# Scores of k over sixteen places of the array, v loaded in smaller pieces, and a new order table

## The chip, the cores and the metric

The kernel runs on one core of a Trainium2 chip. The metric is device time in microseconds for one execution. Before the change it is 266.17 us, the median of 3 runs (265.9 to 266.24). The engines are named as the profile names them: PE (TensorE's matmuls), PEld (its weight loads), DVE (VectorE), ACT (ScalarE), POOL (GpSimd) and SP (SyncE, which here only issues DMAs).

## The reference

Two layers follow one another. First a Nystrom attention over q, k and v, each of 8 batches, 8 heads, 576 tokens and 64 dimensions; then a normalised two-layer MLP with a residual.

```python
q_lm = q.reshape(B, H, 32, 18, D).mean(axis=3)      # 32 landmarks
k_lm = k.reshape(B, H, 32, 18, D).mean(axis=3)
A, Bm, C = sm(q, k_lm), sm(q_lm, k_lm), sm(q_lm, k)  # softmax of scaled scores
Z = Bm^T / (norm_1(Bm) * norm_inf(Bm))
for _ in range(6): Z = 2 * Z - Z @ Bm @ Z
x = (A @ Z @ C @ v)                                  # heads side by side: 576 x 512
out = x + relu(layernorm(x) * g @ w1) @ w2           # w1: 512 x 2048, w2: 2048 x 512
```

## The kernel before, in words

**Units, sets and streams.** A unit is four heads of one batch, so a batch has two (u = 0, 1). Batch 0 has a path of its own. The others come in sets, each a `Coming` object (line 816): (1,), (2,), (3,4), (5,6) and (7,). In a set the units are numbered w = 0, 1, ..., and two neighbours form a pair: one pair in a set of one batch, two in a set of two. For each set q, k and v are loaded by SP into `stg` tiles (line 917; a ring of six tiles), cast to 16 bits by POOL or ACT into `nat` or `natv` (line 924), turned by DVE into `xT` (line 965) and summed to landmarks `lm`. Then `attention2` (line 1082) runs: landmark products and scores of k (`products_k`, line 1022, tiles `psb` and `psec`), their exponentials by ACT and a transpose by DVE (`scores_k`, line 1041, tiles `ec` and `ecT`), scores of q (`scores_q`, line 1058, tile `psea`), the product of the scores of k with v (line 1125, tile `pscv`), six steps of the iteration for Z, a chain of small matmuls and DVE instructions over the tile `st` (lines 750 and 780), and the normalisation of `ea` by POOL (line 561). The MLP's first layer is cut in 16 chunks a batch (line 1361; four matmuls into `psh`, emptied by ACT or DVE into `hT`); the second layer sums products into `bank` tiles (from batch 4 on by a scheme of seven half-size products, line 1528, with mixed weights `w2mix`).

**Places.** A matmul of 32 rows by 32 columns takes one of sixteen places of the 128 x 128 array, given by its row strip (`rb`) and its column strip (`cb`). The row strip is where the data lie; the column strip is where the result is put in PSUM's partitions, and the kernel may choose it if what reads the result agrees. Matmuls in different places can run beside each other; in one place they follow one another. In `products_k` strip p of unit w goes to column strip p if w is even and to (p + 2) mod 4 if it is odd, for both values of r (lines 1030 to 1038). In `scores_q` the column depends on r too, and x is the outermost loop.

**Loads of v.** The unit with even w is loaded by one DMA (`load`, line 315). The one with odd w (sets after (1,)) is loaded by three (`load_swapped`, line 322): 128 rows for slot 0 and two of 64 rows for slot 1, so that the two halves of the partitions are exchanged. SP's queue also carries the stores of finished blocks (line 1269), and each DMA uses one of eight semaphores in turn.

**Order.** The program is laid out by a planner that runs while it is built. `Clock` (line 85) guesses when each instruction would end; `run` (line 1774) picks the next step among five streams: 0 attentions, 1 totals, 2 first layers, 3 first rows, 4 second layers. `help_out` (line 1646) puts in side work: 5 jobs (DVE's turns and sums), 6 measuring, 7 centering of w1, 8 and 9 mixing of matrices, 10 casts, 11 loads. The table `AFTER` (line 1715) overrules the guesses: `(0, 17): (4, 30)` means that step 17 of the attentions waits until the second layers have taken 30 steps. Each engine executes its instructions in the order thus fixed.

Of the kernel before, what the change touches and what calls it, by code (L numbers as in the profile page):

```python
# [10 lines left out]
FP32 = mybir.dt.float32  # L11
UINT32 = mybir.dt.uint32
AF = mybir.ActivationFunctionType
ALU = mybir.AluOpType
AX = mybir.AxisListType

P = 128
# [3 lines left out]
def kernel(  # L21
# [12 lines left out]
    B, H, S, D = q.shape  # L34
# [4 lines left out]
    LM = 32  # L39
# [4 lines left out]
    NJ = 9  # L44
# [11 lines left out]
        name=nc.get_next_instruction_name(), act_func_set_id=6, ins=[], outs=[]))  # L56
# [28 lines left out]
    class Clock:  # L85
# [71 lines left out]
        def note(self, i):  # L157
            e = str(i.engine).rsplit(".", 1)[-1]
            outs = [a.bass_ap for a in i.outs if hasattr(a, "bass_ap")]
            ins = [a.bass_ap for a in i.ins if hasattr(a, "bass_ap")]  # L160
            size = [[k for _, k in a.ap] for a in outs + ins]
            count = []
            for dims in size:
                n = 1
# [4 lines left out]
            writes = [n for a in outs for n in keys_of(a)]  # L169
            ready = 0.0  # L170
            for n in reads:
                t, who = self.wrote.get(n, (0.0, e))
                if who != e or e != "PE":
                    ready = max(ready, t + (self.WAY if who != e else 0.0))
                if n.startswith("psm"):
                    t, who = self.used.get(n, (0.0, e))
# [7 lines left out]
            if type(i).__name__ == "InstDMACopy":  # L184
                start = max(self.free[e], ready)
                self.free[e] = start + (580 if e == "SP" else 100)
                half_ = size[0][0] == 64 and any(n.startswith("stg") for n in writes)
                self.wire = (max(start + 1650, self.wire)
                             + count[0] * size[0][0] * 4 / (150.0 if half_ else 385.0))
                self.loads = self.loads[-24:] + [(start, self.wire)]  # L190
# [61 lines left out]
    def keep(ins):  # L252
        tc.keep_in_program_order(ins)
        clock.note(ins.ins)
        return ins
# [38 lines left out]
    stage = Ring(name="stage", bufs=6)  # L294
# [27 lines left out]
    def load_swapped(src, b, u, queue):  # L322
        t = stage.tile([P, 2, NJ, D], FP32, name="stg", tag="stg")
        heads = src[b, 4 * u:4 * u + 4].rearrange("h (t j) d -> h t j d", j=NJ)
        keep(queue.dma_start(out=t[:, 0, :, :], in_=heads[1:3].rearrange("h t j d -> (h t) j d")))
        for e in range(2):
            keep(queue.dma_start(out=t[ts(1 - e, 64), 1, :, :], in_=heads[3 * e]))
        return t

    raw, nat_tiles, natv_of = {}, {}, {}  # L330
# [7 lines left out]
    for u in range(U):  # L338
# [21 lines left out]
        out=pairs16[:], in_=pm16[:].rearrange("p (e l) -> p e l", e=2)[:, :, None, :]  # L360
# [358 lines left out]
    def softmax_of(psb, W, whole_=False):  # L719
        rsum = asm.tile([P, W], FP32, name="rsum", tag="rsum")  # L720
        dve.tensor_reduce(out=rsum[:], in_=psb[:], axis=AX.X, op=ALU.add)
        rcr = asm.tile([P, W], FP32, name="rcr", tag="rcr", bufs=1)
        dve.reciprocal(out=rcr[:], in_=rsum[:])
        st = asm.tile([P, W, (5 if whole_ else 2) * LM], FP16, name="st", tag="st")
        dve.tensor_tensor(out=st[:, :, -LM:], in0=psb[:],
                          in1=rcr[:, :, None].broadcast_to([P, W, LM]), op=ALU.mult)
        bmT = asm.tile([P, W, LM], FP16, name="bmT", tag="bmT")
        dve.transpose(bmT[:], st[:, :, -LM:])
        if whole_:
            dve.tensor_tensor(  # L730
                out=st[:, :, 0:P].rearrange("p w (h l) -> p w h l", l=LM),
                in0=bmT[:, :, None, :].broadcast_to([P, W, 4, LM]),
                in1=heads_of[0][:, None, :, None].broadcast_to([P, W, 4, LM]), op=ALU.mult)
        return st, bmT

    def whole_gram(psse_, st):
# [79 lines left out]
    class Coming:  # L816
# [100 lines left out]
        def load(self, i, queue=nc.sync):  # L917
            nm, w = self.parts[i]
            b, u = self.units[w]
            src = {"q": q, "k": k, "v": v}[nm]  # L920
            self.stg[i] = stage.pin(load_swapped(src, b, u, queue) if nm == "v" and self.swapped(w)
                                    else load(src, b, u, queue))

        def cast(self, i, by_act=False, part=None):
# [94 lines left out]
                    self.lm[nm, 2 * y + x] = lm[:, ds(4 * i + 2 * x, 2), :, :].rearrange(  # L1019
                        "p r h (l x) -> p r (h l) x", x=2)  # L1020

    def products_k(pair, lm, xT, psb):
        tiles = {w: ps2.tile([P, 2, 512], FP32, name="psec", tag="p2") for w in pair}
        for w in pair:
            for x in range(2):
                for p_ in range(4):
                    rows, r = ts(p_, 32), p_ % 2
                    MM(psb[rows, w, :], lm["q", w][rows, r, :, x], lm["k", w][rows, r, :, x],
                       rb=32 * p_, cb=32 * p_, start=(x == 0), stop=(x == 1), skip=True)
        for r in range(2):  # L1030
            for x in range(2):
                for w in pair:
                    for p_ in range(4):
                        rows = ts(p_, 32)
                        cb = 32 * ((p_ + 2 * (w % 2)) % 4)
                        MM(tiles[w][ds(cb, 32), r, 0:NJ * LM], lm["q", w][rows, r, :, x],
                           xT["k", w][rows, r, :, :, x], rb=32 * p_, cb=cb,
                           start=(x == 0), stop=(x == 1), skip=True)
        return tiles
# [42 lines left out]
    def attention2(bs, c):  # L1082
        units, lm, xT = c.units, c.lm, c.xT
        W = len(units)
# [9 lines left out]
        for y in range(W // 2):  # L1094
            pair = (2 * y, 2 * y + 1)
            yield lambda: clock.both(0.0 if mine else banks.next(), clock.calm(64), aexp.next("e", 4),
                                     clock.at(*c.lm_tiles[y], *[xT["k", w] for w in pair]))
            if y == 0:
                psb = p1([P, W, LM], "psb")
            tiles = products_k(pair, lm, xT, psb)  # L1100
            if y == W // 2 - 1:
                act(psb[:], psb[:], AF.Exp, scale=sc_B)
                st, bmT = softmax_of(psb, W, whole_)
            ecT[pair[0]], ecT[pair[1]] = scores_k(pair, tiles)
            aprep.unpin(*[xT["k", w] for w in pair])
            for w in pair:
                aexp.pin(ecT[w])
# [538 lines left out]
    def help_out(hurry=False):  # L1646
# [66 lines left out]
    begun_first = [0]  # L1713

    AFTER = {
# [14 lines left out]
    }  # L1730
    taken = [0] * 12
    JOB, MEASURE, CENTER, MIX, MIX_W2, CAST, LOAD = range(5, 12)
# [137 lines left out]
```

## Time and profile before

| | |
|---|---|
| median of the runs | 266.17 us |
| the profiled execution | 266.21 us |
| its span (first to last instruction on the core) | 264.5 us |
| busy: PE, DVE, ACT, POOL | 253.4, 207.8, 172.7, 136.9 us |
| scores of k, `psec` | 224 matmuls, 7 pairs |
| scores of q, `psea` | 224 matmuls, 7 pairs |
| DMAs that load v, sets (1,) to (7,) and batch 0 | 10 whole, 6 of 128 rows, 12 of 64 rows |
| DMA, mean over the span | 176 GB/s |

The span is what the profile's views cover; the execution's time holds 1.71 us more. Rows of the view by time give start, length, engine, line, operation, output and inputs, shape and count. A PE row's end is modelled, and matmuls overlap, so the start of the next instruction is the better mark of what a group costs. Nearly all instructions carry line 302 or 308, the helpers that record them, so they are told apart by the names of their tiles. The granted clock of TensorE was 1.00 throughout.

### The profile page before, as it was taken

Reading aid. Unit: us, or ns where it says so; the run is one execution under the profiler, and the core shown is the slowest. Engines: PE = TensorE matmul, PEld = TensorE weight load, DVE = VectorE, ACT = ScalarE, POOL = GpSimd, SP = SyncE. Lnnn points to the kernel's source line nnn. Section 1 sums busy time; section 2 is a strip of 40 time slices with the busy share of each in tenths; the row PEclk is TensorE's granted clock in tenths of the full one; section 3 lists DMA queues with packets and bytes.
Section 4 is the critical chain, followed back from the end, with each engine's and each line's share of the span. In section 5 each row is a group of like instructions: output and inputs, shape, how many; then the busy total and the mean of one; then the engine's idle time right before and its main releaser. Section 6 shows DMA issues by size and latency. Waiting matters only on the chain.

```text
span 264.5 us, 8154 instructions
## 1 busy us (share of the span) xinstructions
PE 253.4 (96%) x3351; PEld 167.9 (63%) x3351; DVE 207.8 (79%) x465; ACT 172.7 (65%) x333; POOL 136.9 (52%) x163
## 2 busy tenths in 40 slices
PE   7799988999899999999999999999999999999994
PEld 6545754556355674446655556677877875788883
DVE  2567964999979987988997974969798758977662
ACT  2488986548686987478787777677576845864000
POOL 5188779999572889989999915600000005000000
PEclk9999999999999999999999999999999999999999
DMA  7999999999794899965803011110060006100605
GB/s 249 372 398 377 387 388 388 346 327 285 251 304 136 272 332 365 266 211 147 267 12 72 11 43 32 42 40 4 0 160 1 4 22 144 39 0 2 159 17 184
DMA packets 23565, 46.67 MB, mean 176 GB/s; under 512 B 2404, under 2 KB 2664, under 8 KB 23528
## 3 DMA queue, kind: packets, MB, share of 16 engines
q1 hardware_dynamic: 23048, 45.49, 53.2%
q10 hardware_dynamic: 480, 0.66, 0.7%
q8 instruction: 26, 0.43, 0.6%
q14 instruction: 11, 0.09, 0.1%
HBM read 36.70 MB, written 9.44 MB: 174 GB/s over the span
## 4 chain that ended last, share of the span: by engine, by line
PE 81%; DVE 10%; DMA 3%; ACT 2%; issue 1%; SPq 1%; DVEq 0%
PE bank L308 54%; PE psh L308 21%; DMA stg<-in_k_dram 3%; DVE m L302 2%; PE pscv L308 2%; DVE w L302 2%; PE psd L308 2%; DVE xblk L302 1%; DVE six L302 1%; PE psea L308 1%; PE psec L308 1%; DVE part L302 1%; ACT lns L302 1%; DVE xT L302 1%; DVE st L302 1%
## 5 line engine op out<-in xcount | busy, mean ns | idle before, releaser
L308 PE MATMUL bank<-w,hT 128*128 128x512 f16 (+3 forms) x528 | 109.7, 334 | 0.0
L302 ACT ACTIVATE hT<-psh 128x576 f16<-128x576 f32 x121 | 75.7, 654 | 24.0 <-PE psh L308 22.7
L308 PEld LDWEIGHTS <-hT 128*128 128x128 f16 x656 | 61.0, 98 | 31.2 <-issue 6.4
L308 PE MATMUL psh<-ea,m 128*128 128x288 f16 x512 | 78.7, 286 | 0.4 <-DVE ea L302 0.3
L308 PEld LDWEIGHTS <-m 128*128 128x128 f16 x512 | 49.0, 98 | 19.7 <-issue 2.8
L302 DVE SCALAR_TENSOR_TENSOR xblk<-bank,rstd,xblk 128x256 f32<-128x256 f32 (+2 forms) x77 | 39.0, 541 | 12.5 <-PE bank L308 12.4
L302 POOL TENSOR_TENSOR ea<-ea,lns 128x576 f16<-128x576 f16 x14 | 17.9, 1285 | 52.0 <-ACT lns L302 51.4
L302 POOL CAST nat<-stg 128x1152 f16<-128x1152 f32 x24 | 27.9, 1182 | 8.9 <-DVE xT L302 6.8
L302 POOL CAST natv<-stg 128x1152 f16<-128x1152 f32 (+1 forms) x17 | 19.3, 1162 | 14.7 <-DMA stg<-in_v_dram 8.1
L302 DVE BATCH_NORM_STATS2 six<-xblk 128x6 f32<-128x512 f32 x36 | 24.2, 674 | 1.6 <-ACT xblk L302 1.6
L302 DVE STREAM_TRANSPOSE xT<-nat 128x576 uint32<-128x576 uint32 x28 | 21.3, 760 | 0.0
L302 DVE SCALAR_TENSOR_TENSOR st<-st,bank 128x128 f16<-128x128 f16 (+3 forms) x36 | 13.2, 366 | 9.6 <-PE bank L308 9.2
L302 ACT COPY xblk<-bank 128x512 f32<-128x512 f32 (+1 forms) x29 | 16.6, 593 | 3.4 <-PE bank L308 2.7
L308 PE MATMUL bank<-w2mix 128*128 128x256 f16 x128 | 17.9, 273 | 0.0
L308 PE MATMUL bank<-w2mix,hT 128*128 128x256 f16 x128 | 16.1, 273 | 0.0
L302 ACT CAST m<-bank 128x512 f16<-128x512 f32 x16 | 9.3, 590 | 8.8 <-PE bank L308 8.7
L302 ACT ACTIVATE lns<-psd 128x576 f32<-128x576 f32 x16 | 10.3, 646 | 7.3 <-PE psd L308 7.1
L308 PEld LDWEIGHTS <-st 32*32 32x32 f16 (+1 forms) x380 | 6.9, 90 | 12.3 <-DVE st L302 7.7
L302 DVE TENSOR_REDUCE part<-xT 128x32 f16<-128x576 f16 x20 | 14.3, 742 | 0.2
L308 PE MATMUL bank<-zcbd,ea 128*128 128x256 f16 x80 | 14.2, 273 | 0.0
L302 POOL TENSOR_TENSOR asum<-nat 128x512 f32<-128x512 f16 x10 | 12.3, 1226 | 3.2 <-ACT nat L302 2.6
L308 PEld LDWEIGHTS <-w2mix 128*128 128x128 f16 x128 | 12.4, 98 | 2.1 <-issue 0.2
(130 smaller groups left out, 369.1 us busy)
## 6 DMA issues: line engine op xcount, KB each, us to landing
stg<-in_q_dram SPq DMA_DIRECT2D x16, 576.0 KB, 6.4
stg<-in_k_dram SPq DMA_DIRECT2D x16, 576.0 KB, 6.0
out_dram<-xblk SPq DMA_DIRECT2D x66, 128.0 KB, 2.4
wstg<-in_moe_w_ch_dram SPq DMA_DIRECT2D x16, 512.0 KB, 7.6
stg<-in_v_dram SPq DMA_DIRECT2D x10, 576.0 KB, 7.4
stg<-in_v_dram SPq DMA_DIRECT2D x6, 288.0 KB, 5.9
stg<-in_v_dram SPq DMA_DIRECT2D x12, 144.0 KB, 5.5
out_dram<-xblk ACTq DMA_DIRECT2D x4, 128.0 KB, 2.9
```

The source lines that it names most:

```text
L302: return lambda *args, **kw: keep(getattr(self.engine, op)(*args, **kw))
L308: keep(nc.tensor.matmul(o, l, r, start=start, stop=stop, tile_position=(rb, cb), skip_group_check=(skip or cb != 0)))
```

## The change

Three things change. In `products_k` the loops over r and x change places, for all sets; and in the sets from (3,4) on ("turned") the column strip is also moved by r, so that a pair uses all sixteen places. The partitions in which the scores of slot r = 1 land are then other ones, so v's slot 1 is loaded to match, in pieces of 32 rows: a unit with u = 0 by five DMAs (one of 128 rows, four of 32), one with u = 1 by six (two of 64 rows, four of 32). In the two sets that iterate on whole 128 x 128 matrices, (2,) and (7,), the mask that spreads the softmax into a block-diagonal matrix is `mask4` (heads in order) in place of `heads_of[0]` (heads 1 and 2 exchanged). The planner's clock takes DMAs of 32 rows as slow ones, as it does those of 64, and `AFTER` is replaced: 72 entries in place of 59, 13 of them the same as before.

```diff
-                half_ = size[0][0] == 64 and any(n.startswith("stg") for n in writes)
+                half_ = size[0][0] <= 64 and any(n.startswith("stg") for n in writes)
...
+    TURNED = 3
+
+    def load_turned(src, b, u, queue):
+        t = stage.tile([P, 2, NJ, D], FP32, name="stg", tag="stg")
+        heads = src[b, 4 * u:4 * u + 4].rearrange("h (t j) d -> h t j d", j=NJ)
+        if u == 0:
+            keep(queue.dma_start(out=t[:, 0, :, :], in_=heads[0:2].rearrange("h t j d -> (h t) j d")))
+        else:
+            for e in range(2):
+                keep(queue.dma_start(out=t[ts(e, 64), e, :, :], in_=heads[1 - e]))
+        for e in range(2):
+            rows, slot = (64 * e, 1) if u == 0 else (64 * (1 - e), e)
+            for half in range(2):
+                keep(queue.dma_start(out=t[ds(rows + 32 * half, 32), slot, :, :],
+                                     in_=heads[2 + e][ds(32 * (1 - half), 32)]))
+        return t
...
-                in1=heads_of[0][:, None, :, None].broadcast_to([P, W, 4, LM]), op=ALU.mult)
+                in1=mask4[:, None, :, None].broadcast_to([P, W, 4, LM]), op=ALU.mult)
...
-            self.stg[i] = stage.pin(load_swapped(src, b, u, queue) if nm == "v" and self.swapped(w)
+            self.stg[i] = stage.pin(load_turned(src, b, u, queue) if nm == "v" and self.bs[0] >= TURNED
+                                    else load_swapped(src, b, u, queue) if nm == "v" and self.swapped(w)
                                     else load(src, b, u, queue))
...
-        for r in range(2):
-            for x in range(2):
+        for x in range(2):
+            for r in range(2):
                 for w in pair:
                     for p_ in range(4):
                         rows = ts(p_, 32)
-                        cb = 32 * ((p_ + 2 * (w % 2)) % 4)
+                        cb = 32 * (p_ ^ 2 * (w % 2) ^ (r if turned else 0))
                         MM(tiles[w][ds(cb, 32), r, 0:NJ * LM], lm["q", w][rows, r, :, x],
                            xT["k", w][rows, r, :, :, x], rb=32 * p_, cb=cb,
                            start=(x == 0), stop=(x == 1), skip=True)
...
-            tiles = products_k(pair, lm, xT, psb)
+            tiles = products_k(pair, lm, xT, psb, bs[0] >= TURNED)
...
-        (0, 95): (2, 110), (0, 104): (4, 513), (0, 112): (4, 558), (0, 116): (4, 584),
+        (0, 45): (4, 153), (0, 64): (4, 196), (0, 80): (4, 267), (0, 95): (4, 335),
+        (0, 99): (4, 463), (0, 104): (4, 513), (0, 112): (4, 559), (1, 5): (4, 94),
...
+        (2, 94): (4, 256), (2, 106): (4, 336), (2, 109): (4, 339), (2, 117): (4, 383),
+        (2, 121): (4, 378), (2, 132): (4, 476), (2, 133): (4, 477), (2, 137): (4, 488),
+        (2, 138): (4, 493), (2, 139): (4, 497), (2, 141): (4, 512), (2, 144): (4, 579),
```

More of the change, by code (lines that the diff above doesn't have):

```diff
@@ L1020, in spread, with products_k @@
                         "p r h (l x) -> p r (h l) x", x=2)
-    def products_k(pair, lm, xT, psb):
+    def products_k(pair, lm, xT, psb, turned):
         tiles = {w: ps2.tile([P, 2, 512], FP32, name="psec", tag="p2") for w in pair}
```

25 rows, old and new, of the table AFTER are left out of this document.

## Prediction, made before the result was known

> **What bounds the kernel now.** I read the page first (busy shares, then the chain that ended last), then the table by stretches of time, then the waits of TensorE's weight loads from 60 us on.
>
> ```profile
> span 264.5 us, 8154 instructions
> PE 253.4 (96%) x3351; PEld 167.9 (63%) x3351; DVE 207.8 (79%) x465; ACT 172.7 (65%) x333; POOL 136.9 (52%) x163
> ...
> PE 81%; DVE 10%; DMA 3%; ACT 2%; issue 1%; SPq 1%; DVEq 0%
> ```
>
> ```profile
> 50.00:75.00 25.00, 23.76 (x264) 13.64 (x263) 24.39 (x48) 17.99 (x35) 21.33 (x24) 1.00 0.91 282
> 75.00:100.00 25.00, 25.00 (x282) 15.55 (x279) 21.78 (x47) 20.10 (x39) 16.52 (x18) 1.00 0.81 269
> 100.00:125.00 25.00, 24.78 (x466) 13.05 (x465) 21.93 (x48) 17.41 (x39) 23.14 (x26) 1.00 0.75 241
> ...
> 200.00:225.00 25.00, 24.98 (x341) 18.38 (x340) 19.01 (x46) 15.34 (x32) 3.56 (x3) 1.00 0.20 47
> ```
>
> ```profile
> PEld L308 <- DVE st L302: 4.7, 11, 1.7
> ```
>
> The columns of the stretches are length, busy PE, PEld, DVE, ACT and POOL (with counts), granted clock, DMA share and GB/s. PE is 96% busy, and 81% of the chain is PE. From 50 to 75 us DVE is the full engine (24.39 of 25 us); from 75 us on PE has hardly a gap, at a granted clock of 1.00. The last row says that in these 200 us the weight loads waited 4.7 us in 11 places for `st`, the chain of small inverse iterations. So a microsecond taken out of PE after 75 us is worth nearly a microsecond, unless it is taken out just ahead of one of those waits.
>
> **The change, part by part: the scores of k.** The five pairs of units that are turned (two of set (3,4), two of (5,6), one of (7,)) run here, `psec` being their tile; the `bank<-lm` rows are the 16 landmark products ahead of them.
>
> ```profile
> 98.79 0.23 PE L308 MATMUL bank<-lm 32*32 32x32 f16 x9
> 98.86 0.30 PE L308 MATMUL psec<-xT,lm 32*32 32x288 f16 x1
> ...
> 98.87 0.30 PE L308 MATMUL psec<-xT,lm 32*32 32x288 f16 x1
> ...
> 98.91 0.68 PE L308 MATMUL psec<-xT,lm 32*32 32x288 f16 x28
> ```
>
> ```profile
> 138.28 0.27 PE L308 MATMUL bank<-lm 32*32 32x32 f16 x16
> 138.39 0.76 PE L308 MATMUL psec<-xT,lm 32*32 32x288 f16 x32
> ```
>
> ```profile
> 201.55 0.77 PE L308 MATMUL psec<-xT,lm 32*32 32x288 f16 x32
> ```
>
> A group of 32 lasts 99.59 - 98.86 = 0.73, 0.76 and 0.77 us. Before, unit w uses the places (p, p) or (p, p^2): eight of the sixteen, four matmuls one behind the other in each. Turned, r moves the column too: sixteen places, two matmuls in each. The trace has that very pattern already: `psea` (the scores of q) is 32 matmuls of the same 32x288 form over all sixteen places, x outermost.
>
> ```profile
> 104.53 0.47 PE L308 MATMUL psea<-xT,lm 32*32 32x288 f16 x32
> ```
>
> ```profile
> 150.63 0.24 PE L308 MATMUL bank<-st 32*32 32x64 f16 x8
> 150.76 0.53 PE L308 MATMUL psea<-xT,lm 32*32 32x288 f16 x20
> ```
>
> Alone it takes 0.47 us. With small matmuls directly ahead it ends at 151.29, 0.66 after the first of these started; for `psec` the same measure is 99.59 - 98.79 = 0.80, and 139.15 - 138.28 = 0.87. So one pair saves between 0.14 (0.80 - 0.66) and 0.30 (0.77 - 0.47). `psec` keeps its small matmuls ahead, but in four places only, and the other twelve are free at once, so I take 0.22, the middle. Five pairs: 5 x 0.22 = **1.1 us**, with ends 0.7 and 1.5. All five lie after 75 us.
>
> The Trainium skill has a rule against this (TensorEngine Tiling (Array Packing), Restrictions and Gotchas, Gotcha 1): different row tiles cannot access the same PSUM bank simultaneously. In `products_k` the four row strips of one unit write one bank, and the first four `psec` matmuls (the first and the last of them are the rows at 98.86 and 98.87) start within 0.02 us of each other, so the trace speaks against it. What it would give is the last rival below.
>
> In sets (1,) and (2,) only the order of r and x changes: the same eight places with four matmuls in each. The exponentials wait for a unit's last matmul either way. I count nothing; the ends are minus and plus 0.1 us, since these two groups lie where DVE is the full engine.
>
> **The mask.** In batches 2 and 7 one operand of one DVE instruction becomes another tile of 128x4 floats, read with the same broadcast.
>
> ```profile
> 203.09 0.43 DVE L302 TENSOR_TENSOR st<-bmT,heads 128x256 f16<-128x256 f16 x1
> ```
>
> Same shape, same type: 0.43 us stay 0.43. Nothing, with ends of 0.05 us either way.
>
> **The loads of v.** For sets from (3,4) on an even unit goes from one DMA to five, an odd one from three to six. Set (3,4) has two of each: 8 issues become 22. Its SP queue and what POOL does with the data:
>
> ```profile
> 71.57 0.55 SPq L317 DMA_DIRECT2D stg<-in_v_dram  x1
> 72.41 0.35 SPq L325 DMA_DIRECT2D stg<-in_v_dram  x1
> 72.81 1.15 SPq L327 DMA_DIRECT2D stg<-in_v_dram  x2
> 74.53 1.13 SPq L1274 DMA_DIRECT2D out_dram<-xblk  x2
> 75.76 0.53 SPq L317 DMA_DIRECT2D stg<-in_v_dram  x1
> 79.39 0.35 SPq L325 DMA_DIRECT2D stg<-in_v_dram  x1
> 79.79 1.14 SPq L327 DMA_DIRECT2D stg<-in_v_dram  x2
> 81.03 1.38 SPq L1274 DMA_DIRECT2D out_dram<-xblk  x2
> 85.26 2.51 SPq L317 DMA_DIRECT2D stg<-in_k_dram  x2
> ```
>
> ```profile
> 87.32 4.49 POOL L302 CAST natv<-stg 128x1152 f16<-128x1152 f32 x4
> 93.25 3.43 POOL L302 CAST nat<-stg 128x1152 f16<-128x1152 f32 x3 [1.45 <-DVE xT L302]
> ...
> 115.75 1.28 POOL L302 TENSOR_TENSOR ea<-ea,lns 128x576 f16<-128x576 f16 x1 [0.24 <-PE bank L308]
> ```
>
> ```profile
> L327 SPq DMA_DIRECT2D stg<-in_v_dram x12: 495/587/1471, 46.0 to 125.9; - x12
> ...
> DMA to landing us min/median/max: 3.3/5.5/8.4
> ```
>
> No DMA of 32 rows is in the trace; the nearest is that of 64 rows, 0.59 us of SP's queue at the median and 5.5 us to its landing. Fourteen more are 14 x 0.59 = 8.3 us of queue. Between 71.57 and the last v issue SP has gaps of 0.3, 0.6, 0.1 and 3.1 us, 4.1 together, so the last piece goes out about 4.2 us later: from 80.4 (79.79 + half of 1.14) to 84.6, and lands at 90.1. POOL's fourth cast of v starts at 87.32 + 3 x 1.12 = 90.7. It fits by 0.6 us. The two stores at 74.53 and 81.03 and the load of k at 85.26 go behind the pieces; the stores are waited for by nobody near, and the k is needed by POOL from 93.25 on. If that cover goes, with the longest landing of 8.4 us, the cast is 2.3 us late, and then the 1.45 us that POOL idled ahead of 93.25 takes most of it. Behind this cast stand POOL's casts and sums and the two normalisations of batch 3, the second at 115.75, whose result PE uses first here:
>
> ```profile
> 121.00 0.65 PE L308 MATMUL psh<-ea,m 128*128 128x288 f16 x4
> ```
>
> That is 121.00 - 117.03 = 4 us later. So up to 1.45 + 4 = 5.4 us of delay costs PE nothing, and beyond it a microsecond costs a microsecond. Set (5,6) has more room: its last v is issued and cast here,
>
> ```profile
> 107.36 1.14 SPq L327 DMA_DIRECT2D stg<-in_v_dram  x2
> ```
>
> ```profile
> 120.26 4.47 POOL L302 CAST natv<-stg 128x1152 f16<-128x1152 f32 x4
> ```
>
> 12 us apart; and the last v issue of all, at 125.9 by the row of L327, is that of batch 7, whose scores run at 201.55. I count the loads at nothing.
>
> **The new table.** It holds no work, only which stream may go on when. Taken against the kernel's own order before, it keeps most steps where they were, holds a few dozen back by one to a dozen steps of the second layer, and frees some. The largest holds are in the first layers (step 117 waits for 15 more second-layer steps, step 139 for 12). A second-layer step is one matmul:
>
> ```profile
> 202.25 1.27 PE L308 MATMUL bank<-w2mix 128*128 128x256 f16 x10
> ```
>
> and ten of them take 1.27 us where one alone lasts 0.27, a pitch of 1.00 / 9 = 0.11 us. Moving it costs PE nothing; only a wait that is opened or closed counts. With PE already full after 75 us there is little to close: some of the 4.7 us above. From both sides I bound it by minus 1 us (a fifth of the 4.7) and plus 2 us (rival 3 with twelve chunks), and take nothing, since the order is mostly the old one.
>
> **Sum.** 264.5 - 1.1 = 263.4 us of span. The profiled execution took 266.21 us, 1.71 more than its span, and the median of the runs is 266.17, the same within 0.02%. 263.4 + 1.7 = **265.1 us**, 0.4% faster; its own range by the ends of the first term is 264.7 to 265.5.
>
> **Rivals.** A measurement of this kernel tells about 0.2% (0.5 us) from no change.
> 1. The saved time is lost in waits for `st`. At 201.55 softmax's DVE chain starts from the landmark products, not from `psec`, and ends at 203.09 + 0.43; PE would arrive 0.22 us sooner and wait as much longer. If three of the five places are like that, 0.4 us remain: 265.8 us. For it: PE waits there now; against it: other products can be put in between. 13%.
> 2. The new order also closes waits, some 0.8 us of the 4.7: 264.3 us. For it: the many one-step moves near the `st` steps; against it: nothing in the trace shows which. 15%.
> 3. Slower: the order bunches first-layer chunks. A chunk takes PE 0.49 us, and the ACT instruction that empties its tile 0.65:
>
> ```profile
> L302 ACT ACTIVATE hT<-psh 128x576 f16<-128x576 f32 x121 | 75.7, 654 | 24.0 <-PE psh L308 22.7
> ```
>
> ```profile
> 208.19 0.49 PE L308 MATMUL bank<-w2mix 128*128 128x256 f16 x3
> 208.51 0.65 PE L308 MATMUL psh<-ea,m 128*128 128x288 f16 x4
> ```
>
> (The chunk's row is 0.65 to its last end; the next instruction starts 0.49 after it.) Two such tiles exist. Now, near 208 us, a chunk has three products of the second layer beside it, and PE does not wait. Held back without them, each chunk costs 0.16 us. Ten bunched chunks (1.6 us) undo the gain and pass the 0.2%; sixteen, a whole batch, give 265.1 + 2.6 = 267.7; at about twelve 267.0. 12%.
> 4. Slower: v too late in set (3,4), the mechanism above. It decides from 5.4 + 1.6 = 7 us of delay on, say 268. 4%, since the sum has it 0.6 us early.
> 5. The change does not do what it says: the four row strips of one bank take turns. A step in a place now takes (0.73 - 0.30) / 3 = 0.14 us; eight in turn per bank last 7 x 0.14 + 0.30 = 1.3 us instead of 0.75, and five pairs lose 2.7: 268.9 us. Against it stand the four starts above. 3%.
>
> **How the numbers follow.** Forecast 53%, and the rest as given. Faster: the forecast, rival 2, and none of rival 1: 68%. Within 0.2%: rival 1 and a little of rival 3: 14%. Slower: what is left of 3, with 4 and 5: 18%. The range leaves out the better part of rivals 4 and 5 and the ends of 2 and 3: 263.9 to 267.0.
>
> **What would show it.** Right: the five `psec` groups at 0.47 to 0.6 us instead of 0.73 to 0.77, first starts in sixteen places, the exponentials following sooner, PE busy as full as before after 75 us, and a span shorter by their sum. Wrong: POOL idle ahead of `natv` for `stg<-in_v_dram` between 85 and 95 us; PE or its weight loads waiting for ACT (`hT`) or longer for `st`; or `psec` groups still at 0.7 us. A span that changes by much more than five groups can explain is the table's doing.

## The result and the profile after

The changed kernel takes **265.53 us** (median of 19 runs, 264.95 to 266.36) against 266.23 for the kernel before on the same chip (19 runs, 265.88 to 267.02): a ratio of 0.9974, with the interval 0.9966 to 0.9982. That is 0.70 us less; forecast were 265.1, or 1.1 less. The profiled execution took 265.93 us, its span is 264.2.

From the page of the changed kernel, the span, the busy shares and the shares of the chain that ended last:

```profile
span 264.2 us, 8212 instructions
PE 253.6 (96%) x3351; PEld 167.7 (63%) x3351; DVE 209.4 (79%) x466; ACT 173.2 (66%) x333; POOL 136.0 (51%) x162
...
PE 75%; DVE 11%; DMA 8%; ACT 2%; POOL 2%; issue 1%; SPq 0%; DVEq 0%
```

Its stretches of time, with the columns as before (length, busy PE, PEld, DVE, ACT, POOL, granted clock, DMA share, GB/s):

```profile
50.00:75.00 25.00, 24.36 (x267) 13.73 (x265) 24.46 (x49) 17.59 (x35) 22.56 (x25) 1.00 0.91 286
75.00:100.00 25.00, 24.90 (x277) 15.49 (x276) 21.67 (x46) 20.50 (x40) 15.86 (x16) 1.00 0.78 251
100.00:125.00 25.00, 25.00 (x480) 13.12 (x478) 22.72 (x50) 18.59 (x39) 21.60 (x24) 1.00 0.71 200
...
150.00:175.00 25.00, 24.07 (x353) 15.26 (x353) 19.29 (x39) 18.42 (x32) 14.26 (x13) 1.00 0.19 44
...
200.00:225.00 25.00, 24.97 (x343) 18.41 (x341) 18.33 (x44) 15.38 (x32) 3.57 (x3) 1.00 0.21 48
```

Before, the fourth of these was:

```profile
150.00:175.00 25.00, 25.00 (x402) 15.55 (x400) 19.13 (x41) 18.06 (x32) 11.50 (x10) 1.00 0.19 44
```

Two of these stretches are not what the sum had. From 50 to 75 us PE is busier (24.36 us, 23.76 before). From 150 to 175 us, where nothing of the change was expected, PE lacks 0.93 us. TensorE's waits from 60 us on say what it waited for, its weight loads first:

```profile
PEld L308 <- DVE st L302: 3.8, 10, 1.0
```

```profile
PE bank L308 <- DVE xblk L302: 0.9, 1, 0.9
```

The weight loads' longest wait for `st` has gone from 1.7 to 1.0 us, and PE's wait for `xblk` is new. The scores of k did what the diff says; here are the first rows of the landmark products and the last row of `psec` in one group each of sets (3,4) and (7,), with the product that follows the latter:

```profile
98.61 0.24 PE L308 MATMUL bank<-lm 32*32 32x32 f16 x9
...
98.72 0.53 PE L308 MATMUL psec<-xT,lm 32*32 32x288 f16 x21
...
201.95 0.24 PE L308 MATMUL bank<-lm 32*32 32x32 f16 x9
...
202.05 0.55 PE L308 MATMUL psec<-xT,lm 32*32 32x288 f16 x22
202.53 0.72 PE L308 MATMUL bank<-w2mix 128*128 128x256 f16 x5
```

The measure of the prediction, from the first of the small matmuls to the last end, is 99.25 - 98.61 = 0.64 us, where it was 0.80; the two parts of the pair overlap as `psea` does.

### The profile page after: what moved, and what is told of

Same layout as the page of the kernel before. It is cut to its first block, busy times and chain, and to the rows that moved or that the text cites. A ratio compares the mean times of both kernels' runs of the same rounds, so it can differ in the third digit from the quotient of the medians.

```text
span 264.2 us, 8212 instructions
## 1 busy us (share of the span) xinstructions
PE 253.6 (96%) x3351; PEld 167.7 (63%) x3351; DVE 209.4 (79%) x466; ACT 173.2 (66%) x333; POOL 136.0 (51%) x162
## 4 chain that ended last, share of the span: by engine, by line
PE 75%; DVE 11%; DMA 8%; ACT 2%; POOL 2%; issue 1%; SPq 0%; DVEq 0%
PE bank L308 49%; PE psh L308 20%; DMA stg<-in_k_dram 4%; DMA wstg<-in_moe_w_ch_dram 4%; DVE m L302 2%; DVE w L302 2%; PE pscv L308 2%; PE psd L308 2%; DVE xblk L302 1%; DVE six L302 1%; DVE part L302 1%; POOL w L302 1%; PE psea L308 1%; ACT lns L302 1%; DVE xT L302 1%
## 5 line engine op out<-in xcount | busy, mean ns | idle before, releaser
L302 ACT ACTIVATE hT<-psh 128x576 f16<-128x576 f32 x119 | 74.3, 653 | 20.9 <-PE psh L308 19.2
L302 POOL CAST nat<-stg 128x1152 f16<-128x1152 f32 x23 | 26.9, 1186 | 12.9 <-DVE xT L302 7.1
L302 POOL TENSOR_TENSOR asum<-asum 128x256 f32<-128x256 f32 (+1 forms) x20 | 12.8, 641 | 1.6
```

The lines of the kernel that those rows point to most:

```text
L302: return lambda *args, **kw: keep(getattr(self.engine, op)(*args, **kw))
```

## The theories and the experiments

The question is whether the 0.70 us are the 1.1 us of the places with a little lost, or a sum of larger parts. Three parts can be set apart: the **places**, the **loads** of v (both together are the **work**), and the **order** that the table makes. The obstacle is that the planner lays out the program by its clock's guesses, so a change of work also changes the order. So in eight of the eleven experiments the clock is shown the other variant: for a product in `products_k`, `clock.seen` holds the place that the clock is to believe, and `unseen(...)` issues loads of one kind while the clock notes the cost of another. The order of the instructions on DVE, ACT and POOL is then exactly that of the kernel before ("old order") or of the changed one ("new order"), and on PE too except inside the groups of the scores of k (one of the eight keeps the order of the run that holds the measuring step). All times are medians. The ratios are to the kernel before on the same chip, which took 266.21 us beside the first four experiments, 266.30 beside the two with the loads of set (7,), the one that holds the measuring step and the one with loops and mask, and 266.19 beside the rest. The changed kernel was timed only in the runs of the result, against 266.23, so a difference to its 265.53 also holds what chips differ by. What a run changes of the computation is said in its expectation.

### Work in the old order, and the new order without the work

**The new places and loads in the old order.** On the kernel before, with its table and its mask, and with the loops over r and x exchanged as in the change:

```diff
-                        cb = 32 * ((p_ + 2 * (w % 2)) % 4)
+                        cb = 32 * (p_ ^ 2 * (w % 2) ^ (r if turned else 0))
+                        clock.seen = (32 * p_, 32 * ((p_ + 2 * (w % 2)) % 4))
...
-            self.stg[i] = stage.pin(load_swapped(src, b, u, queue) if nm == "v" and self.swapped(w)
+            self.stg[i] = stage.pin(unseen(load_turned, src, b, u, queue, "swapped" if self.swapped(w) else "plain")
+                                    if nm == "v" and self.bs[0] >= TURNED
```

> The order of all engines' instructions is that of before; only the places of the scores of k in the five turned pairs and the loads of v are the changed ones (no new table, old mask). Theory A (the gain is the five shorter groups of scores, 0.16 us each in the two profiles, and nothing else adds up): 0.8 us faster than before, ratio 0.9970. Rival B (the new order makes the gain, the saved PE time falls into waits): within 0.2 us of before. Rival C (the smaller pieces of v cost something that the order repays): between 0.8 us faster and no change, and slower than the run with the places alone.

Measured: 265.19 us, ratio 0.9955 (0.9936 to 0.9975). The work alone gives 1.02 us, a little more than theory A has.

**The new places alone in the old order**: the same, without the second hunk.

> As before in order and loads; only the places of the scores of k are changed in the five turned pairs. The second half of v's rows then meets the wrong scores: the product with v is of the same size but not the reference's. Theory A: 0.8 us faster than before. Rival B: within 0.2 us. Rival C: faster than the run with the loads too.

Measured: 266.03 us, ratio 0.9995 (0.9975 to 1.0015): 0.18 us less, and the interval covers no change, so rival B by the time. In the profiled execution the five groups are 0.88 us shorter than before; 0.2 of that go into a longer stop of PE near 111 us and 0.2 into a wait at set (7,), both shown below.

**The new order without the work.** On the changed kernel, with its table and mask, but old places and old loads:

```diff
-                        cb = 32 * (p_ ^ 2 * (w % 2) ^ (r if turned else 0))
+                        clock.seen = (32 * p_, 32 * (p_ ^ 2 * (w % 2) ^ (r if turned else 0)))
+                        cb = 32 * ((p_ + 2 * (w % 2)) % 4)
...
-            self.stg[i] = stage.pin(load_turned(src, b, u, queue) if nm == "v" and self.bs[0] >= TURNED
+            self.stg[i] = stage.pin(unseen(load_swapped if self.swapped(w) else load, src, b, u, queue, "turned")
+                                    if nm == "v" and self.bs[0] >= TURNED
```

> The order of all engines' instructions is that of the changed kernel, with the new mask; the scores of k lie in the eight old places and v is loaded as before. Theory A: the order alone is worth nothing or less (it ends a wait near 70 us and opens one near 171 us): 266.2 to 266.5. Rival B: 265.5, as the changed kernel. In the profile the wait of PE for xblk near 171 us should be there again, about 1 us.

Measured: **265.03 us**, ratio 0.9949 (0.9933 to 0.9966). The order alone gives 1.18 us; with the work that it was made for, the kernel is 0.5 us slower than without. Both expected times missed, and the wait for `xblk` near 171 us, expected here, is not there: it is the changed kernel's. So the work alone is worth 1.02 us and the order alone 1.18, and both together 0.70: the parts do not add up.

**The new order and the new loads with the old places**: the first hunk of that diff alone.

> The changed kernel with the scores of k in the eight old places, v loaded in the new pieces, so that the product with v is of the same size but not the reference's. Theory A: 0.8 us slower than the changed kernel, the same as the run with the old loads too. Rival B: as the changed kernel, 265.5. Rival C: slower than the run with the old loads.

Measured: 265.96 us, ratio 0.9988 (0.9972 to 1.0004): rival C.

What follows: in the new order the loads cost 265.96 - 265.03 = 0.93 us, and the places give 265.96 - 265.53 = 0.43. (In the old order the loads give 266.03 - 265.19 = 0.84, and the places 0.18.) Each of these medians is uncertain by 0.3 to 0.5 us, so the traces have to say where. These are the starts (us) of the `psec` groups from the second on, and the span:

| kernel | 2nd | 3rd | 4th | 5th | 6th | 7th | span |
|---|---|---|---|---|---|---|---|
| before | 67.53 | 98.86 | 101.84 | 138.39 | 142.34 | 201.55 | 264.5 |
| new order, old work | 66.96 | 98.37 | 101.36 | 137.68 | 141.16 | 201.07 | 263.3 |
| new order, new loads, old places | 67.13 | 98.53 | 101.52 | 137.85 | 141.33 | 202.28 | 264.5 |
| changed | 67.27 | 98.68 | 101.50 | 137.87 | 141.19 | 202.01 | 264.2 |

Between the second and the third of these kernels the distance stays at 0.16 or 0.17 us up to the 6th group, and is 1.21 at the 7th: **the loads' cost is one event between 141 and 202 us**, long after the last load of v. It is PE's new wait. Here is PE in the changed kernel, and then in the new order with the old work:

```profile
170.75 0.39 PE L308 MATMUL psm<-w,zt 64*32 64x512 f16 x1
172.07 0.37 PE L308 MATMUL bank<-w,zt 64*32 64x512 f16 x1 [0.93 <-DVE xblk L302]
```

```profile
170.86 0.39 PE L334 MATMUL psm<-w,zt 64*32 64x512 f16 x1
171.13 0.37 PE L334 MATMUL bank<-w,zt 64*32 64x512 f16 x1
```

The second group of eight matmuls follows the first after 0.27 us in one and 1.32 us in the other. `xblk` is written by DVE. DVE and POOL at that place in the changed kernel, and DVE's instructions on `w2mix` there (minimum, median and maximum in ns):

```profile
169.21 2.15 DVE L302 TENSOR_TENSOR w2mix<-hT 128x1024 f16<-128x1024 f16 x2
171.28 0.74 DVE L302 SCALAR_TENSOR_TENSOR xblk<-bank,rstd,xblk 128x512 f32<-128x512 f32 x1
```

```profile
169.78 1.04 POOL L302 COPY hT<-hT 128x1024 f16<-128x1024 f16 x1 [1.47 <-PE bank L308]
```

```profile
L302 DVE TENSOR_TENSOR w2mix<-hT x2: 693/1114/1536, 169.2 to 169.8; 128x1024 f16<-128x1024 f16 x2
```

and the same in the new order with the old work:

```profile
169.12 1.29 DVE L328 TENSOR_TENSOR w2mix<-hT 128x1024 f16<-128x1024 f16 x2
170.33 0.75 DVE L328 SCALAR_TENSOR_TENSOR xblk<-bank,rstd,xblk 128x512 f32<-128x512 f32 x1
```

```profile
169.88 1.44 POOL L328 COPY hT<-hT 128x1024 f16<-128x1024 f16 x1 [1.47 <-PE bank L334]
```

The second of DVE's two mixing instructions takes 1.54 us instead of 0.69, and POOL's copy 1.04 instead of 1.44. In the changed kernel the DVE instruction starts at 169.21 + 2.15 - 1.54 = 169.82, 0.04 us after POOL's copy; in the other at 169.12 + 1.29 - 0.69 = 169.72, 0.16 us before it. Whoever starts first runs at its own speed, and the other is held up: DVE by 0.85 us, or POOL by 0.40. The Trainium skill (SBUF — State Buffer, SBUF: two separate sides) says this: DVE and GpSimd share a pair of ports as an exclusive lock, for a DVE instruction with two inputs in SBUF against a GpSimd instruction that reads SBUF, and the one that starts first has it for the whole instruction. The trace agrees, 1.54 against 0.69 us. The one that is held ends close to where it would if it began at the other's end: DVE at 169.21 + 2.15 = 171.36 against 169.78 + 1.04 + 0.69 = 171.51, and POOL at 169.88 + 1.44 = 171.32 against 169.12 + 1.29 + 1.04 = 171.45.

Why DVE is late by just that much is in its queue ahead of the first mixing instruction. The last statistics instruction there, in the changed kernel, is this:

```profile
168.91 0.18 DVE L302 BATCH_NORM_AGGREGATE stats<-six 128x2 f32<-128x6 f32 x1
```

Instructions that only wait for semaphores, between it and the mixing, in the changed kernel and in the other (count, ns, first and last start):

```profile
L302 DVEq EVENT_SEMAPHORE  x3: 50/50/50, 168.9 to 169.1; - x3
```

```profile
L328 DVEq EVENT_SEMAPHORE  x1: 50/50/50, 169.0 to 169.0; - x1
```

They are 0.10 us apart, so two more are 0.2 us. (In the old order the same waits cost nothing: a copy of 0.69 us stands ahead of them, and the mixing starts 0.61 us after its start with the old loads and with the new.) By the kernel's code, `w2mix` is a tile of the ring `stg` (tag `stg`), and the tile that was there before held v of set (7,). It is now filled by five or six DMAs on semaphores of their own, and the first instruction that writes over it must wait for all of them, some 35 us after the last was issued. That is the theory to test; the rival is that the loads, in flight longer, delay something of set (7,) by themselves.

### Where the loads' cost comes from

**The changed kernel, with the v of set (7,) alone loaded as before:**

```diff
+            self.stg[i] = stage.pin(unseen(load_swapped if self.swapped(w) else load, src, b, u, queue, "turned")
+                                    if nm == "v" and self.bs[0] == 7
```

> The changed kernel in its own order, but v of set (7,) is loaded as before, by one and three DMAs (the second half of its rows meets the wrong scores; all sizes stay). Theory D (the six DMAs of a v tile make DVE wait for each of their semaphores before it writes that tile's buffer again as w2mix; that sets the second mixing instruction behind POOL's copy of hT, DVE is held for 0.8 us, and PE waits 1.0 us for xblk near 171 us): fewer semaphore waits before the first w2mix at 169 us, both mixing instructions together 1.3 us instead of 2.15, no wait of PE near 171 us, 1.0 us faster than the changed kernel, 264.5. Rival E (the wait comes from the loads of the other sets, which move the DMAs and POOL between 70 and 125 us): no difference, 265.5, with the wait.

Measured: 264.62 us, ratio 0.9937 (0.9915 to 0.9959): 0.91 us less than the changed kernel, as theory D has it. Two waiting instructions are left of the three; DVE and POOL:

```profile
168.68 1.29 DVE L328 TENSOR_TENSOR w2mix<-hT 128x1024 f16<-128x1024 f16 x2
```

```profile
169.34 1.53 POOL L328 COPY hT<-hT 128x1024 f16<-128x1024 f16 x1 [1.48 <-PE bank L334]
```

DVE's second instruction starts at 168.68 + 1.29 - 0.69 = 169.28, ahead of the copy at 169.34, and takes 0.69 again. PE does not wait.

**The opposite: the new order and old work, with the v of set (7,) alone in pieces:**

```diff
-                                    if nm == "v" and self.bs[0] >= TURNED
+                                    if nm == "v" and TURNED <= self.bs[0] < 7
```

> The run of the new order with the old work, where only v of set (7,) is loaded in the new pieces (which meet the wrong scores; all sizes stay). Theory D: the wait near 171 us comes back, the mixing pair takes 2.15 us again, and the time goes from 265.0 to 266.0. Rival E: 265.0, no wait.

Measured: 265.17 us, ratio 0.9956 (0.9940 to 0.9972). **The expectation failed**: the wait at PE did not return, though the three waiting instructions did. The rows show why:

```profile
169.71 1.29 DVE L328 TENSOR_TENSOR w2mix<-hT 128x1024 f16<-128x1024 f16 x2
```

```profile
170.31 1.60 POOL L328 COPY hT<-hT 128x1024 f16<-128x1024 f16 x1 [1.48 <-PE bank L334]
```

DVE's second instruction starts at 170.32, 0.01 us after POOL's copy, and still it is POOL that is held (1.60 us). So the three waits put DVE at the edge of the collision, but a few hundredths of a microsecond decide it: 0.01 us late is won, 0.04 us late (the changed kernel, and the one with old places) is lost. By the profile's start times, then, the first to start is not always the one that has the ports. The last statistics instruction starts here at

```profile
169.44 0.18 DVE L328 BATCH_NORM_AGGREGATE stats<-six 128x2 f32<-128x6 f32 x1
```

Counted from its start in each kernel, POOL's copy always comes at the same time, and the waits alone move DVE:

| kernel | waiting instructions | DVE's second mixing, us | POOL's copy, us | held |
|---|---|---|---|---|
| new order, old work | 1 | 0.71 | 0.87 | POOL |
| changed, old loads of (7,) | 2 | 0.81 | 0.87 | POOL |
| old work, new loads of (7,) | 3, one of them of 21 ns instead of 50 | 0.88 | 0.87 | POOL |
| changed | 3 | 0.91 | 0.87 | DVE |
| new order, new loads, old places | 3 | 0.91 | 0.87 | DVE |

So the mechanism of theory D stands, with 0.03 us between won and lost; its forecast for this run failed by the one shorter wait.

**The changed kernel with the measuring step held again.** The old table held measuring step 22 until attention step 96; the new table has no such entry. Measuring is what DVE does right ahead of the mixing: the statistics of a finished block. One entry puts it behind it; the orders of PE, DVE and ACT change by it between 168 and 198 us (36 places of DVE's, 14 of ACT's):

```diff
+        (6, 22): (4, 299),
```

> The changed kernel with one entry more in the table: measuring step 22 waits until the second layers have taken 299 steps (the table before the change held it too), so that DVE mixes w2mix 0.9 us earlier, ahead of POOL's copy of hT. Theory D: no wait of PE near 171 us, 264.4 to 264.8. Rival E: the wait stays, 265.5. If another wait opens in its place, in between.

Measured: **263.95 us**, ratio 0.9908 (0.9879 to 0.9937), less than both kernels and less than expected. DVE, POOL and the stretch from 150 to 175 us:

```profile
167.61 1.28 DVE L302 TENSOR_TENSOR w2mix<-hT 128x1024 f16<-128x1024 f16 x2
...
169.41 0.74 DVE L302 SCALAR_TENSOR_TENSOR xblk<-bank,rstd,xblk 128x512 f32<-128x512 f32 x1
```

```profile
169.19 1.20 POOL L302 COPY hT<-hT 128x1024 f16<-128x1024 f16 x1 [1.47 <-PE bank L308]
```

```profile
150.00:175.00 25.00, 25.00 (x365) 16.36 (x364) 19.30 (x39) 17.97 (x33) 12.16 (x11) 1.00 0.19 44
```

The two mixing instructions are over at 168.89, before POOL's copy starts, with the new loads and all their waits in place, and PE is busy all of the 25 us. So in this order the loads cost nothing by themselves; their cost is the collision. That this edit gives 1.58 us in the medians where the wait is 0.93 is not all explained. Its span is 1.7 shorter, and only 1.12 of that arise between the 6th and the 7th `psec` group, where the edit acts; 0.41 are there already at the 2nd, and 0.18 more arise between the 4th and the 5th, before it has done anything.

**The same with the old places**, to have the worth of the places once more:

```diff
+        (6, 22): (4, 299),
...
-                        cb = 32 * (p_ ^ 2 * (w % 2) ^ (r if turned else 0))
+                        clock.seen = (32 * p_, 32 * (p_ ^ 2 * (w % 2) ^ (r if turned else 0)))
+                        cb = 32 * ((p_ + 2 * (w % 2)) % 4)
```

> The run with measuring step 22 held, where only the scores of k are put back into the eight old places in the five turned pairs (v's pieces then meet the wrong scores; all sizes stay). Theory A, now for the places alone: in an order without the collision the places are worth their five shorter groups, less what the waits take: 0.6 to 0.8 us slower than with the new places, 264.6 to 264.8. Rival B: within 0.2 us, 264.0.

Measured: 265.12 us, ratio 0.9960 (0.9949 to 0.9972), so the places give 1.17 us here, more than expected, in the medians of two chips; the spans are 263.3 and 262.5, 0.8 apart. The starts of the `psec` groups are 67.06, 98.46, 101.45, 137.78, 141.25, 201.09 against 66.86, 98.27, 101.10, 137.29, 140.61, 200.31: the distance is 0.20 and 0.19 up to the first turned pair, then grows by 0.14 to 0.16 with each pair, to 0.78 at the 7th. The 0.20 at the start are scatter of the two executions, so about 0.6 us of the 0.8 are the places'.

### The loops, the mask, the loads and the table by themselves

**The kernel before with the loops exchanged and the new mask:**

```diff
-        for r in range(2):
-            for x in range(2):
+        for x in range(2):
+            for r in range(2):
...
-                in1=heads_of[0][:, None, :, None].broadcast_to([P, W, 4, LM]), op=ALU.mult)
+                in1=mask4[:, None, :, None].broadcast_to([P, W, 4, LM]), op=ALU.mult)
```

> The kernel before with two small parts of the change alone: r and x exchanged in the scores of k (the same eight places) and the new mask in batches 2 and 7. All theories: no change, within 0.2 us of before.

Measured: 266.21 us, ratio 1.0000 (0.9981 to 1.0019). No change, within 0.2%.

**The new loads alone in the old order** (the second hunk of the first experiment alone):

> The kernel before in its own order, where only v of the sets from (3,4) on is loaded in the new pieces (which meet the wrong scores; all sizes stay). Theory F (the pieces stretch SP's issues, so that the DMA engines have a gap near 108 us, PE's next instructions are there in time, and the stop of PE in the product with v near 111 us goes): no stop of PE near 111 us, 0.4 to 0.6 us faster than before, 265.7. Rival C (pieces cost, or do nothing by themselves): as before or slower, with the stop.

Measured: 265.81 us, ratio 0.9999 (0.9980 to 1.0018). The median is 0.38 us less, but the interval covers no change, and the profiled execution was among the longer ones (266.54). This was inconclusive on time. It shows one thing: in the old order PE stops near 111 us, in the product with v, when the loads are the old ones, and does not when they come in pieces. (With loops and mask exchanged the stop is there too, 0.09 us.) The kernel before, then the new places in the old order, then the new loads in the old order:

```profile
111.45 0.60 PE L308 MATMUL pscv<-natv,ecT 64*64 64x130 f16 x28 [0.22 <-issue]
```

```profile
111.28 0.60 PE L334 MATMUL pscv<-natv,ecT 64*64 64x130 f16 x28 [0.43 <-issue]
```

```profile
111.04 1.25 PE L334 MATMUL pscv<-natv,ecT 64*64 64x130 f16 x72
```

The DMA traffic differs just ahead of it. The stretch from 108 to 109 us in the new places in the old order, and in the new places and loads in the old order:

```profile
108.00:109.00 1.00, 1.00 (x47) 0.51 (x19) 0.97 (x3) 0.56 (x2) 0.92 (x2) 1.00 1.10 420
```

```profile
108.00:109.00 1.00, 1.00 (x48) 0.51 (x19) 0.97 (x3) 0.56 (x2) 0.92 (x2) 1.00 0.07 14
```

With the pieces the DMA engines are nearly idle there (0.07 of their time, 1.10 without). So in the old order the pieces remove a stop: from before to the first experiment PE gains 0.41 us at 111 us. "issue" names no releaser. A candidate is in the trace: some of its DMA packets are loads of instructions, 16 KB each, for an engine that it does not name. One ends at 109.81 us in the kernel before and at 109.70 with the new places in the old order, and PE goes on at 111.45 and 111.28, 1.64 and 1.58 us later. With the new loads in the old order it ends at 109.28, and PE passes the place without a stop. That fits instructions which arrive late because the data hold them up, but no run changes that alone, and it is not shown. That the DMA engines are full is not enough by itself, as this stretch of the new order with the old work shows:

```profile
108.00:109.00 1.00, 1.00 (x20) 0.41 (x5) 0.97 (x3) 0.79 (x2) 0.92 (x2) 1.00 1.01 359
```

The DMA engines are nearly as full there, the load of instructions ends at 108.87, and PE does not stop. So the cause stays open; and as the stop is gone in the new order with the old loads as well, the pieces and the order remove the same stop, and it counts only once.

**The changed kernel with the old table** (the order is not kept here; the planner makes its own):

```diff
-        (0, 17): (4, 31), (0, 23): (4, 77), (0, 34): (2, 51), (0, 35): (4, 106),
+        (0, 17): (4, 30), (0, 19): (2, 44), (0, 23): (4, 76), (0, 27): (4, 78), (0, 34): (2, 51),
...
```

> The changed kernel with the table of before: same work as the changed kernel, but the planner, which now counts shorter scores and longer loads, lays it out with entries made for the old work. Theory G (the entries fit only the order they were made for): slower than the changed kernel, by 0.5 us or more, 266.0 to 268. Rival: as the run of the new work in the old order, 265.2.

Measured: 273.23 us, ratio 1.0249 (1.0227 to 1.0271), 7.0 us more than before and past the expected 268. The stretch from 100 to 125 us and PE's longest wait in this kernel:

```profile
100.00:125.00 25.00, 22.16 (x433) 10.28 (x431) 18.39 (x42) 11.00 (x27) 20.60 (x23) 0.93 0.78 238
```

```profile
PE bank L308 <- DVE st L302: 3.9, 4, 1.8
```

PE lacks 2.8 us in that stretch alone, with the granted clock at 0.93. Here the old table does not carry over to the new work.

## Why the prediction was right, and where it was not

The total was right, 265.53 within 263.9 to 267.0 and faster by more than 0.2%; the sum behind it was not. It had one term of 1.1 us. The runs show three, two of which it had at nothing, and that the total came out near the forecast is luck: a gain of 1.18 and a cost of 0.93 nearly cancel.

| step | forecast, us | measured, us |
|---|---|---|
| places, five pairs | -1.1 (-0.7 to -1.5) | groups -0.82; net -0.43 (new order) and about -0.6 (measuring held, spans without the start) |
| loads of v | 0 | +0.93 in the new order, by the collision of DVE and POOL |
| loops, mask | 0 | 0.00 |
| new table | 0 (-1 to +2) | -1.18 |
| sum | -1.1 | -1.18 + 0.93 - 0.43 = -0.68 |

The measured terms are differences from one run to the next, so their sum closes by construction, and they hold for this sequence alone (first the order, then the loads, then the places). In the old order the work as a whole gives 1.02 us, close to the 1.1, but not as the sum had it: by the medians 0.84 of it are the loads', and the places alone give 0.18.

- **Places.** The mechanism was right and the size too large. From the first `psec` start to the next instruction the five groups took 0.65, 0.65, 0.70, 0.65 and 0.70 us before and take 0.50, 0.51, 0.50, 0.51 and 0.51 now: 0.82 us together, 0.16 a pair where 0.22 was taken. (In the new order with the old places they take 0.65 to 0.66, so 0.74 us of it are the places'.) I had taken the middle between the time of `psea` alone and with small matmuls ahead of it; the group is at the second of these (0.66 by the same measure, 0.64 here), so the lower end was the answer. The small matmuls sit in four places only, and still cost as much.
- **Rival 1** (the saved time lost in waits for `st`) is true for one of the five pairs. The new places in the old order, at set (7,):

```profile
201.00 0.54 PE L334 MATMUL psec<-xT,lm 32*32 32x288 f16 x32
...
203.01 0.29 PE L334 MATMUL bank<-st 128*128 128x128 f16 x2 [0.24 <-DVE st L328]
```

  The pair has become 0.22 us shorter, and PE waits 0.24 us at the next step, where it waited 0.02 before (the prediction took it that PE waits there already). In the new order 0.15 us are given back at the same place, against the kernel with the old places. The other four keep their gain there, though one is lost again near 111 us in the profiled execution of the changed kernel, where 16 weight loads for `st` take 0.35 us instead of 0.17.
- **Loads of v.** What was worked out held in its result: the data are there when POOL casts them. SP's queue, and POOL's casts:

```profile
84.75 1.97 SPq L343 DMA_DIRECT2D stg<-in_v_dram  x4
```

```profile
86.97 4.48 POOL L302 CAST natv<-stg 128x1152 f16<-128x1152 f32 x4
```

```profile
stg<-in_v_dram SPq DMA_DIRECT2D x40, 72.0 KB, 3.0
```

  The last piece goes out by 86.7 (84.6 forecast), but a piece takes 1.82 / 4 = 0.46 to 0.49 us of the queue and lands after 3.0 us at the median, not 5.5, so it is there by 89.7 and the fourth cast starts at 86.97 + 3 x 1.12 = 90.3 without a wait. Rival 4 is out. **The step that failed is "I count the loads at nothing"**: it followed the data to their reader, and not the buffer to its next writer, which now waits for six DMA semaphores where the same order with the old loads has it wait for two.
- **The table. The step that failed is "take nothing, since the order is mostly the old one".** Rival 2 was the case, with a size (1.18) past its 0.8 and past the bound of minus 1, which came from the waits for `st` alone. The largest wait that went is this one, in the kernel before; then the stretch from 67 to 75 us before and after:

```profile
70.98 0.19 PE L308 MATMUL bank<-st,bones 128*128 128x64 f16 x1 [0.69 <-DVE st L302]
```

```profile
67.00:75.00 8.00, 6.76 (x142) 3.17 (x141) 7.60 (x21) 5.80 (x14) 5.04 (x7) 1.00 0.76 234
```

```profile
67.00:75.00 8.00, 7.45 (x147) 3.62 (x146) 7.70 (x20) 5.56 (x14) 6.27 (x8) 1.00 0.77 254
```

  PE has 0.69 us more work in these 8 us, as also in the new order with the old work. Another 0.22 are the stop at 111 us. Most of the rest lies earlier still, in these two waits of the kernel before, of which the new order (here with the old work) has only the second left:

```profile
45.56 0.24 PE L308 MATMUL pszt<-st,cv 32*32 32x32 f16 x16 [0.34 <-DVE st L302]
46.23 0.22 PE L308 MATMUL pszc<-cv,st 32*32 32x64 f16 x8 [0.43 <-ACT lns L302]
```

```profile
45.83 0.22 PE L334 MATMUL pszc<-cv,st 32*32 32x64 f16 x8 [0.30 <-ACT lns L328]
```

  That is 0.34 + 0.43 - 0.30 = 0.47 us. The three make 0.69 + 0.22 + 0.47 = 1.38, and some 0.15 of small new gaps of PE between 50 and 100 us have to be taken off; the spans differ by 1.2. The prediction ruled the stretch up to 75 us out as DVE's, and looked for waits to close only after it.
- **Rival 3** (bunched chunks) shows nowhere; in no stretch of the new order after 75 us does PE wait for `hT`. **Rival 5** and the rule of the Trainium skill behind it (TensorEngine Tiling (Array Packing), Restrictions and Gotchas, Gotcha 1) are out: four row strips that write one bank would have made a pair 1.3 us long, and it is 0.57 to 0.59.
- The profiled execution is only 0.28 us below the one of before where the medians differ by 0.70. The changed kernel's was already 0.31 us behind the new order with the old work at the 2nd `psec` group, ahead of every turned pair: single executions scatter by that much, which is why the distances above are taken from group to group.

## What to carry to other kernels

When a load is cut into more DMAs, follow its buffer as well as its data: the next writer of that buffer, however much later, waits for every one of them, and 0.2 us on a queue can decide which of two engines goes first. Where a schedule is fitted by hand to one variant of the work, run the schedule without the work and the work without the schedule before crediting either; here the new order alone, and the new work alone, were each worth more than the whole change. A time that comes out as forecast does not show that its terms did.

## What the runs showed of the hardware

- A DVE instruction on 128x1024 16-bit elements with two inputs takes 0.69 us, and 1.54 when a POOL copy of the same size started 0.04 us ahead of it. When DVE wins, the copy takes 1.44 to 1.60 us instead of 1.04. The edge lies between 0.01 and 0.04 us of DVE's start after POOL's.
- Each further instruction that only waits for semaphores, all of them long signalled, cost 0.10 us ahead of the DVE instruction behind a statistics instruction of 0.18 us; behind a copy of 0.69 us it cost nothing.
- Thirty-two matmuls of 32x288 over sixteen places are followed by the next instruction after 0.50 to 0.51 us, over eight places after 0.65 to 0.70: half the depth in each place saves about a quarter. The four row strips write one bank, and their first matmuls start within 0.02 us of each other.
- A DMA of 32 rows (72 KB) holds SP's queue for 0.46 to 0.49 us in a run of four and lands after 3.0 us at the median; that of 64 rows was at 0.59 and 5.5 in the kernel before.
